# LayerNorm statistics combined on GpSimd instead of VectorE, with the last weight rows loaded twice and a new order of the whole program

## The chip, the cores and the metric

The kernel runs on one core of one Trainium2 chip. The metric is the device time of that core for one execution, in microseconds (us). In the lines of the profile, PE is TensorE's matmuls, PEld its weight loads, DVE is VectorE (called Vector here), ACT is ScalarE, POOL is GpSimd and SP is SyncE, which here only issues DMA. "L783" is line 783 of the kernel.

## The reference

A transformer block on 2048 tokens of width 448, in bf16. The first half is attention over a sliding, dilated window (16 heads of 28, 8 keys at a distance of 2 tokens from each other), the second a gated MLP that mixes tokens with a 2048 x 2048 matrix. Cut to what matters:

```python
def layernorm(x):
    return (x - mean(x)) / sqrt(var(x) + 1e-5)

q, k, v = split(layernorm(A_x) @ A_wqkv)          # 448 -> 3 x 448
logits  = q . k[pos - 2*j] / sqrt(28),  j = 0..7  # masked where pos - 2*j < 0
h       = A_x + (softmax(logits) . v) @ A_wo

z       = gelu(layernorm(h) @ B_w_in)             # 448 -> 1792
z1, z2  = z[:, :896], z[:, 896:]
g       = B_w_sp @ layernorm(z2) + B_b_sp         # mixes the 2048 tokens
out     = h + (z1 * g) @ B_w_out                  # 896 -> 448
```

There are three LayerNorms: LN1 on the input, LN2 on h, and LN3 on z2. The change concerns the first two.

## The kernel before

**Tiles.** The 2048 tokens are 16 blocks of 128. Block u and block u + 8 form unit u, so there are 8 units. In the transposed activations `xh` the first 1024 tokens lie on partitions 0 to 63 and the second 1024 on partitions 64 to 127, each with the 448 channels as seven blocks of 64. A product over 448 channels is therefore seven pairs of 64-row matmuls, one pair member per half, which run side by side on TensorE. So every weight (wqkv, w_in) must lie on both partition halves: it is loaded as three blocks of 128 rows and one of 64 rows, and Vector or ScalarE copy what a half lacks from the other one (`cross`, L569, for V and w_in; the pad copies, L741 to L756, for Q and K, which also spread the heads from 28 to 32 columns).

**A LayerNorm unit** (`ln_unit`, L650) is: `bn_stats` (L656) and `bn_aggr` (L657) on Vector for each of the two blocks; then the reciprocal root `rs`, two operations on GpSimd (add eps, then a power of -1/2; L646, L647) or two on ScalarE (L668, L669); then two normalisations on Vector (L676); then a transpose, either by a DMA on SyncE (L683, LN1 units 0 to 4 and all of LN2) or on TensorE (L692) with an eviction (L700). GpSimd's second operation waits for its first.

`bn_stats` writes six numbers for a row of 448: count, mean and squared deviation of the even elements, and the same of the odd ones. `bn_aggr` combines them into mean and variance.

**Stages.** TensorE first runs 15 filling products on constants (L635). Then q and k are made in chunks of the 1024 paired tokens (L783): chunks 3 and 2 are 128 tokens each (units 7 and 6), chunk 1 is 256 (units 4 and 5), chunk 0 is 512 (units 0 to 3). V (L823) and the attention tiles (nine of 114 tokens, from tile 8 down to 0) follow as their tokens come: logits (L858), exponential on ScalarE (L870), the mask on Vector (L877), row sums (L886), logarithm and scaling on ScalarE (L899, L921), products with V (L911), their eviction with the scaling on Vector (L929), the output product (L964) and the residual addition on Vector (L972), whose result LN2 takes up again. Then come z2 (L984), its gelu on ScalarE (L994), LN3 (L1000 to L1014), z1 (L1028), and to the end the mixing product g (L1064) and the output product (L1093).

**What sets the order.** Nothing is ordered by the hardware or a compiler: the program is a list of tasks (`rs1_4`, `nrm1_12`, `cpk000`, ...), and the table `SEQ` gives for each of the five engines the order in which it issues them. Each engine works its own list in that order and waits at the head of it. `Planner.replay` (L304) steps through the five lists with estimated durations, gives out the eight PSUM banks in that estimated order, and emits the instructions; the class `Sched` adds the semaphores. The planner's constants (durations, DMA rates, what an instruction fetch costs) thus touch the program only through banks and buffers, and through the table.

Of the kernel before, what the change touches and what calls it, by code (L numbers as in the profile page):

```python
# [5 lines left out]
S_TOK = 2048  # L6
# [18 lines left out]
BLK = ((0, 2, 4, 6, 1, 3, 5), (1, 3, 5, 0, 2, 4, 6))  # L25
# [40 lines left out]
)  # L66
NBANKS = 8
NE = 2
NL = 2
NV = 3  # L70
# [125 lines left out]
class Task:  # L196
# [3 lines left out]
    def __init__(self, name, eng, dur, emit, deps=(), acq=(), rel=(), mode=None,  # L200
# [13 lines left out]
        self.setup = 2.0  # L214
        self.waits = []
        self.mark = None
        self.alts = alts
        self.start = self.end = None


# [943 lines left out]
```

## Time and profile before

| | |
|---|---|
| time, three runs | median 241.22 us (241.19 to 241.9) |
| profiled execution | span 241.1 us |
| Vector, share of the span | 59%; 90% or more in 12 of the 40 slices, nine of them from 42 to 96 us |
| GpSimd | 27.1 us busy, 11% |
| DMA | 20.01 MB in 54,628 packets |
| PEclk | 9 (tenths of full speed, 9 is 90% or more) in every slice |

The profile's page has several parts. The first gives the busy time of each engine. The second cuts the span into 40 slices of 6 us and prints the busy share of each engine in tenths, and for DMA also GB/s. The third lists the DMA queues. The fourth is the chain of work that ended last, followed back from the last instruction: each row is a start, a length, and the engine and line, or "issue" where the engine waited for nothing that the profile shows. The fifth gives groups of equal instructions: the row ends in busy time, the mean length of one in ns, and the idle time of the engine just ahead of them. The timeline lists instructions of an engine in order of start: start, length, engine, line, operation, result and operands, and in brackets how long the engine had been idle and what ended that. A row for a tile (for instance `rs`) gives minimum, median and maximum length in ns, then the first and last start. The table by windows gives, for each stretch of time, the busy share of PE and PEld (with the instructions started), then of DVE, ACT and POOL, the granted clock, the share of DMA and its GB/s.

The profiled program has 6691 instructions. Loads take place all through the first half of the span, and DMA is nearly idle for a good part of the second, in which TensorE works on the mixing and output products.

### The profile page before, as it was taken

Reading aid. Unit: us, or ns where it says so; the run is one execution under the profiler, and the core shown is the slowest. Engines: PE = TensorE matmul, PEld = TensorE weight load, DVE = VectorE, ACT = ScalarE, POOL = GpSimd, SP = SyncE. Lnnn points to the kernel's source line nnn. Section 1 sums busy time; section 2 is a strip of 40 time slices with the busy share of each in tenths; the row PEclk is TensorE's granted clock in tenths of the full one; section 3 lists DMA queues with packets and bytes.
Section 4 is the critical chain, followed back from the end, with each engine's and each line's share of the span. In section 5 each row is a group of like instructions: output and inputs, shape, how many; then the busy total and the mean of one; then the engine's idle time right before and its main releaser. Section 6 shows DMA issues by size and latency. Waiting matters only on the chain.

```text
span 241.1 us, 6691 instructions
## 1 busy us (share of the span) xinstructions
PE 234.0 (97%) x3009; PEld 119.8 (50%) x3019; DVE 141.3 (59%) x280; ACT 92.9 (39%) x111; POOL 27.1 (11%) x68
## 2 busy tenths in 40 slices
PE   7898999999999999999999999999999999999995
PEld 2476865455554444454444444444444444444453
DVE  4998954999999999778820050253101436554443
ACT  2898879859899648665630000000000000000000
POOL 6044000002014023105700000000000000000000
PEclk9999999999999999999999999999999999999999
DMA  7927787732303567998535433200000000010122
GB/s 210 331 57 84 117 136 151 140 78 61 44 4 72 108 112 172 181 161 132 113 83 152 90 87 79 52 3 0 0 0 3 0 0 19 19 61 0 38 93 79
DMA packets 54628, 20.01 MB, mean 83 GB/s; under 512 B 46792, under 2 KB 54472, under 8 KB 54600
## 3 DMA queue, kind: packets, MB, share of 16 engines
q1 hardware_dynamic: 53416, 18.61, 37.9%
q10 hardware_dynamic: 1184, 0.98, 1.4%
q8 instruction: 23, 0.38, 0.7%
q14 instruction: 5, 0.04, 0.0%
HBM read 6.37 MB, written 1.84 MB: 34 GB/s over the span
## 4 chain that ended last, share of the span: by engine, by line
PE 85%; DVE 5%; POOL 3%; issue 2%; DMA 2%; ACT 1%; POOLq 1%; ACTq 0%
PE psum L1064 40%; PE psum L783 9%; PE psum L1093 9%; PE psum L984 8%; PE psum L823 5%; PE psum L964 5%; PE psum L1028 4%; PE psum L858 2%; DMA z2p<-in_A_wqkv_dram 2%; POOL rs L647 2%; PE psum L911 1%; DVE x_tm L972 1%; DVE w_in L643 1%; DVE reg L643 1%; PE psum L886 1%
## 5 line engine op out<-in xcount | busy, mean ns | idle before, releaser
L1073 DVE TENSOR_TENSOR ub<-psum,reg 128x512 bf16<-128x512 f32 x28 | 18.9, 688 | 68.4 <-PE psum L1064 66.0
L1064 PE MATMUL psum<-reg,z2p 128*128 128x512 bf16 x220 | 49.4, 379 | 0.2
L1064 PE MATMUL psum<-wspT_lo,z2p 128*128 128x512 bf16 x218 | 48.5, 379 | 0.4 <-DVE z2p L1014 0.2
L1064 PEld LDWEIGHTS psum<-wspT_lo,z2p 128*128 128x128 bf16 x224 | 21.8, 98 | 26.6 <-issue 0.4
L1064 PEld LDWEIGHTS psum<-reg,z2p 128*128 128x128 bf16 x224 | 21.9, 98 | 26.2
L783 PE MATMUL psum<-xh,reg 64*128 64x128 bf16 (+2 forms) x448 | 26.4, 270 | 0.4 <-issue 0.4
L984 PE MATMUL psum<-w_in,xh 64*128 64x448 bf16 x224 | 22.4, 349 | 0.0
L1093 PE MATMUL psum<-reg 128*128 128x448 bf16 (+2 forms) x119 | 22.2, 342 | 0.1
L1028 PE MATMUL psum<-xh,w_in 64*128 64x512 bf16 x196 | 22.0, 376 | 0.0
L656 DVE BATCH_NORM_STATS2 st<-x_tm 128x6 f32<-128x448 bf16 x32 | 19.5, 610 | 3.6 <-DMA x_tm<-in_A_x_dram 3.5
L783 PEld LDWEIGHTS psum<-xh,reg 64*128 64x128 bf16 x448 | 16.8, 94 | 7.9 <-issue 1.4
L641 ACT ACTIVATE reg<-psum 128x896 bf16<-128x896 f32 (+2 forms) x24 | 19.4, 838 | 1.1 <-PE psum L783 0.9
L1000 DVE BATCH_NORM_STATS2 st<-z2p 128x6 f32<-128x448 bf16 x32 | 17.8, 610 | 1.9 <-ACT z2p L994 1.8
L870 ACT ACTIVATE reg<-psum 128x928 bf16<-128x928 f32 x18 | 16.3, 944 | 5.2 <-PE psum L858 5.2
L994 ACT ACTIVATE z2p<-psum 128x896 bf16<-128x896 f32 x16 | 14.2, 918 | 7.6 <-PE psum L984 7.6
L1038 ACT ACTIVATE reg<-psum 128x1024 bf16<-128x1024 f32 x14 | 13.6, 1026 | 8.4 <-PE psum L1028 8.4
L1093 PEld LDWEIGHTS psum<-reg 128*128 128x128 bf16 x119 | 11.4, 98 | 10.4
L646 POOL TENSOR_SCALAR rs<-mv 128x2 f32<-128x2 f32 x19 | 6.5, 342 | 88.9 <-DVE mv L657 72.3
L1103 DVE TENSOR_TENSOR tring<-psum,x_tm 128x448 bf16<-128x448 f32 (+2 forms) x17 | 10.1, 597 | 10.2 <-PE psum L1093 10.0
L984 PEld LDWEIGHTS psum<-w_in,xh 64*128 64x128 bf16 x224 | 10.6, 94 | 10.5 <-issue 0.4
L1028 PEld LDWEIGHTS psum<-xh,w_in 64*128 64x128 bf16 x196 | 9.4, 94 | 11.5 <-ACT reg L1038 0.2
L647 POOL TENSOR_TENSOR rs<-rs,nhalf 128x2 f32<-128x2 f32 x19 | 14.3, 754 | 1.6
(62 smaller groups left out, 202.7 us busy)
## 6 DMA issues: line engine op xcount, KB each, us to landing
x_tm<-in_A_x_dram SPq DMA_DIRECT2D x15, 112.0 KB, 4.9
out_dram<-tring SPq DMA_DIRECT2D x15, 112.0 KB, 1.7
w_in<-in_B_w_in_dram SPq DMA_DIRECT2D x2, 448.0 KB, 4.7
reg<-in_B_w_out_dram SPq DMA_DIRECT2D x1, 784.0 KB, 6.0
z2p<-in_A_wqkv_dram ACTq DMA_DIRECT2D x2, 336.0 KB, 5.5
reg<-in_B_b_sp_dram SPq DMA_DIRECT2D x1, 512.0 KB, 4.6
w_in<-in_B_w_in_dram SPq DMA_DIRECT2D x2, 224.0 KB, 4.7
reg<-in_A_wo_dram SPq DMA_DIRECT2D x4, 98.0 KB
```

What stands on the lines that cost most here:

```text
L641: iss("act", lambda e: e.activation(dst, src, AF.Copy), reads=rd, writes=wr)
L647: iss("pool", lambda e: e.tensor_tensor(dst, dst, nh, ALU.pow), reads=rr + [r_nhalf], writes=rr)
L656: iss("dve", lambda e: e.bn_stats(st[:, b, :], x_tm[:, b, :]), reads=[r_x[b]], writes=[rl[b]])
L783: iss("pe", lambda e, c=c, s=s, gi=gi, lhs=lhs: e.matmul(psum[:, bk[s] * 512 + cw * gi:bk[s] * 512 + cw * gi + cw], lhs, xh[64 * s:64 * s ...
L870: iss("act", lambda e: e.activation(E[:, es[0], 2 * n:2 * n + 2, :], pair_view(lb, 0, 8 * JW), AF.Exp, scale=SCALE), reads=[r_bank[lb[0]], ...
L984: iss("pe", lambda e, k2=k2, c=BLK[s][k2], s=s: e.matmul(psum[:, zb[s] * 512:zb[s] * 512 + D], xh[64 * s:64 * s + 64, c, HX + 128 * u:HX + ...
L994: iss("act", lambda e: e.activation(z2p[:, u:u + 9:8, D * k:D * k + D], pair_view(zb, 0, D), AF.Gelu_apprx_tanh), reads=[r_bank[zb[0]], r_ ...
L1000: iss("dve", lambda e, b=b: e.bn_stats(st3[:, b, k, :], z2p[:, b, D * k:D * k + D]), reads=[r_z2[b][k]], writes=[r_st3[b][k]])
L1028: iss("pe", lambda e, k=k, c=BLK[s][k], s=s: e.matmul(psum[:, bk[s] * 512:bk[s] * 512 + 512], w_in[64 * s:64 * s + 64, k, 128 * f:128 * f ...
L1064: iss("pe", lambda e, b=b: e.matmul(psum[:, gb[0] * 512:gb[0] * 512 + 512], z2p[:, b, 128 * f:128 * f + 128], src[:, b, 512 * (tc % 2):512 ...
L1073: iss("dve", lambda e: e.tensor_tensor(ub[:, us_[0], :], psum[:, gb[0] * 512:gb[0] * 512 + 512], bb[:, 512 * tc:512 * tc + 512], ALU.add), ...
L1093: iss("pe", lambda e, f=f: e.matmul(psum[:, wb[0] * 512 + d0:wb[0] * 512 + d1], z1p[f][:, 128 * m:128 * m + 128], w_out[:, f, d0:d1], star ...
```

## The change

It has four parts.

1. **Statistics.** Vector keeps `bn_stats` for all units, but `bn_aggr` only for units 7 and 6 of LN1 (`AGGR`). For the other six units of LN1 and all eight of LN2, GpSimd combines the six numbers itself: a new function `aggr` of nine operations on 128 x 2 elements, each waiting for the one before. Five combine two tensors (subtract, square, two sums, and the sum of the means), three scale by constants, and the last is the power. So `rs1_0`, `rs1_2` and `rs1_3`, which ScalarE made before with two activations, are GpSimd's too; `rs1_6` is on GpSimd and `rs1_7` on ScalarE.

2. **Weights.** The last 64 rows of each third of wqkv, and of w_in, are loaded twice, once to each partition half. For w_in this is a load of its own over all 1792 columns (`ld_winl`). The cross copies then carry three blocks each way, where one way had four. The four pad copies for Q and K become three: one on all 128 partitions, and one on each half. The order of the channel blocks on the upper half changes with that (`BLK`), and the q and k products read the block that fits their weight.

3. **Constants.** Some memsets move from GpSimd to Vector (pads of Wq, of V, and the zeros under wo); those for the k pads, the ones and the mask band no longer wait for `rs1_7`.

4. **Order.** The planner's constants change, it gets two rules for Vector and GpSimd waiting on each other, and `SEQ` is searched anew. The V products of the first two tiles come ahead of all q and k products (L868 before L828 in the new program, on TensorE's list); x blocks 14, 15, 7 and 6 are loaded first; the weights of V are loaded ahead of those of Q and K; pieces of wo and w_in are loaded later.

The core of the diff (the planner's new durations are left out, and of `SEQ` a line stands for all):

```diff
-BLK = ((0, 2, 4, 6, 1, 3, 5), (1, 3, 5, 0, 2, 4, 6))
+BLK = ((0, 2, 4, 6, 1, 3, 5), (1, 3, 5, 6, 0, 2, 4))
...
-    (23, 29, 26, 28, 31, 24, 27, 25, 30, 55, 48, 85, 87, 73, 86, 330, 384, 366, 348, 402, 420, 438, 456, 341, 413, 395, 359,
+    (26, 31, 29, 27, 28, 88, 90, 30, 89, 44, 58, 51, 76, 70, 64, 82, 330, 384, 348, 366, 420, 456, 402, 438, 395, 359,
...
+AGGR = (7, 6)
+AGT = 2.9
+SPLIT = "q"
...
+        self.blk = 2 if name[:3] in ('nrm', 'cpk', 'cpq') else 0
...
         def w_view(dst, src):
...
-                    (dst[0:64, 3, :], src[384:448], 154.0))
+                    (dst[0:64, 3, :], src[384:448], 200.0), (dst[64:128, 3, :], src[384:448], 200.0))
...
         def cross(name, w, rs, deps, n):
             out = []
-            for h, lo, nb in ((0, 4, 3), (1, 3, 4)):
+            for h in range(2):
                 tk = []
...
+                    copy(tk[0].eng, w[64 * h:64 * h + 64, 4:NC7, :], w[64 - 64 * h:128 - 64 * h, 0:3, :], rs[:-2], [rs[h - 2]])
...
+        def ld_winl():
+            for h in range(2):
+                t_winl.append(dma("sp", "winl%d" % h, lambda e, h=h: e.dma_start(w_in[64 * h:64 * h + 64, 3, :], B_w_in[384:448, :]),
+                                  64 * FH * 4, writes=[r_winl[h]], bw=240.0))
...
+        def aggr(s6, m2, dst, rr):
+            def tt(a, b, c, op):
+                iss("pool", lambda e: e.tensor_tensor(a, b, c, op), reads=rr, writes=rr)
+
+            def ts(a, b, c, d, o1, o2=None):
+                iss("pool", lambda e: e.tensor_scalar(a, b, c, d, o1, o2) if o2 else e.tensor_scalar(a, b, c, None, o1), reads=rr, writes=rr)
+            me, qe, mo, qo = (s6[:, :, n] for n in (1, 2, 4, 5))
+            mean, var = m2[:, :, 0], m2[:, :, 1]
+            tt(var, me, mo, ALU.subtract)
+            tt(var, var, var, ALU.mult)
+            ts(var, var, 0.25 * D, None, ALU.mult)
+            tt(dst, qe, qo, ALU.add)
+            tt(var, var, dst, ALU.add)
+            ts(var, var, 1.0 / D, EPS, ALU.mult, ALU.add)
+            tt(mean, me, mo, ALU.add)
+            ts(mean, mean, 0.5, None, ALU.mult)
+            iss("pool", lambda e: e.tensor_tensor(dst, var, nhalf[:, 0:2], ALU.pow), reads=rr + [r_nhalf], writes=rr)
...
         def ln_unit(u, which, src_deps, ev_deps):
...
+            ag = which == 1 and u in AGGR
...
-                    iss("dve", lambda e: e.bn_aggr(mv[:, b, :], st[:, b, :]), reads=[rl[b]], writes=[rl[b]])
...
+                    if ag:
+                        iss("dve", lambda e: e.bn_aggr(mv[:, b, :], st[:, b, :]), reads=[rl[b]], writes=[rl[b]])
...
-                if tk[0].eng == "pool":
+                if not ag:
+                    aggr(st[:, u:u + 9:8, :], mv[:, u:u + 9:8, :], dst, rr)
+                elif tk[0].eng == "pool":
                     rstd(dst, var, nhalf[:, 0:2], rr)
...
-                for n, (h, q) in enumerate(((0, 0), (0, 1), (1, 0), (1, 1))):
+                for n, (h0, h1, lo, q) in enumerate(((0, 128, 0, 0), (0, 64, 4, 64), (64, 128, 4, 0))):
...
-                                        xh[64 * s:64 * s + 64, c, HX + t0:HX + t0 + cw],
+                                        xh[64 * s:64 * s + 64, b, HX + t0:HX + t0 + cw],
```

**How the lists change.** The rows below are an engine's list in the order of issue: line, operation, result and operands, shape, and how many of them in a row.

ScalarE at its start, before: its loads, then the reciprocal root of unit 7 (L668, L669) and copies of weights (L641).

```order
L553 DMA x_tm<-in_A_x_dram 128x448
L566 DMA z2p<-in_A_wqkv_dram 128x3x448
L566 DMA z2p<-in_A_wqkv_dram 64x448
L566 DMA reg1<-in_A_wqkv_dram 64x448
L566 DMA z2p<-in_A_wqkv_dram 64x448
L508 ACT_TABLE_LOAD
L566 DMA z2p<-in_A_wqkv_dram 128x3x448
L668 ACTIVATE rs1<-mv1,epst 128x2
L669 ACTIVATE rs1<-rs1 128x2
L641 ACTIVATE reg1<-z2p 64x3x8x28
```

In the new program, where they are L712, L713 and L663:

```order
L563 DMA x_tm<-in_A_x_dram 128x448 x2
L518 ACT_TABLE_LOAD
L576 DMA reg1<-in_A_wqkv_dram 64x448
L712 ACTIVATE rs1<-mv1,epst 128x2
L713 ACTIVATE rs1<-rs1 128x2
L663 ACTIVATE reg1<-reg1 64x1344
L663 ACTIVATE xh<-psum 128x7x128 x2
L663 ACTIVATE reg1<-z2p 128x4x8x28
```

ScalarE now issues three loads where it issued six, and its first copies are half of V's weights (64x1344) and the evictions of both transposed units (`xh<-psum`).

GpSimd from the first `rs` on, before: two roots, constants for the k and q pads and the mask band, a third root, and then the constants for the row sums.

```order
L646 TENSOR_SCALAR rs1<-mv1 128x2
L647 TENSOR_TENSOR rs1<-rs1,nhalf 128x2
L646 TENSOR_SCALAR rs1<-mv1 128x2
L647 TENSOR_TENSOR rs1<-rs1,nhalf 128x2
L714 MEMSET reg2 128x8x2
L715 MEMSET reg2 128x4x14
L716 MEMSET reg2 128x8x2
L717 MEMSET reg2 128x8x2
L723 MEMSET mband 128x58
L725 AFFINE_SELECT mband<-mband 64x58
L727 AFFINE_SELECT mband<-mband 64x58
L725 AFFINE_SELECT mband<-mband 64x58
```

In the new program the constants are done, and from the first root (unit 6, with Vector's aggregation) on there stand:

```order
L668 TENSOR_SCALAR rs1<-mv1 128x2
L669 TENSOR_TENSOR rs1<-rs1,nhalf 128x2
L674 TENSOR_TENSOR mv1<-st1 128x2
L674 TENSOR_TENSOR mv1<-mv1 128x2
L677 TENSOR_SCALAR mv1<-mv1 128x2
L674 TENSOR_TENSOR rs1<-st1 128x2
L674 TENSOR_TENSOR mv1<-mv1,rs1 128x2
L677 TENSOR_SCALAR mv1<-mv1 128x2
L674 TENSOR_TENSOR mv1<-st1 128x2
L677 TENSOR_SCALAR mv1<-mv1 128x2
L688 TENSOR_TENSOR rs1<-mv1,nhalf 128x2
L674 TENSOR_TENSOR mv1<-st1 128x2
```

From the third row on this is unit 4 in nine operations, and units 5, 1, 2, 3 and 0 of LN1 follow in the same way, then LN2's units 7, 4, 6, 5, 2, 0, 3 and 1.

Vector inside attention, where LN2 begins, before: statistics (L656) and aggregations (L657) of LN2 among masks (L877), additions (L972), normalisations (L676) and L929 steps.

```order
L929 TENSOR_TENSOR reg2<-psum,reg3 128x2x8x57
L676 TENSOR_SCALAR tring<-x_tm,mv2,rs2 128x2x7x32
L972 TENSOR_TENSOR x_tm<-psum,x_tm 128x2x448
L877 TENSOR_TENSOR reg3<-reg3,mband 128x1856
L972 TENSOR_TENSOR x_tm<-psum,x_tm 128x2x448
L929 TENSOR_TENSOR reg2<-psum,reg3 128x2x8x57
L656 BN_STATS st2<-x_tm 128x6
L657 BN_AGGR mv2<-st2 128x2
L656 BN_STATS st2<-x_tm 128x6
L657 BN_AGGR mv2<-st2 128x2
L656 BN_STATS st2<-x_tm 128x6
L657 BN_AGGR mv2<-st2 128x2
```

In the new program, in the same stretch, where these lines are L697, L922, L1018, L720 and L974:

```order
L922 TENSOR_TENSOR reg3<-reg3,mband 128x1856
L1018 TENSOR_TENSOR x_tm<-psum,x_tm 128x2x448 x2
L974 TENSOR_TENSOR reg2<-psum,reg3 128x2x8x57
L697 BN_STATS st2<-x_tm 128x6 x2
L922 TENSOR_TENSOR reg3<-reg3,mband 128x1856
L697 BN_STATS st2<-x_tm 128x6
L974 TENSOR_TENSOR reg2<-psum,reg3 128x2x8x57
L697 BN_STATS st2<-x_tm 128x6
L720 TENSOR_SCALAR tring<-x_tm,mv2,rs2 128x2x7x32
L697 BN_STATS st2<-x_tm 128x6
L922 TENSOR_TENSOR reg3<-reg3,mband 128x1856
L720 TENSOR_SCALAR tring<-x_tm,mv2,rs2 128x2x7x32
```

The aggregations are gone, and a normalisation (`tring<-x_tm,mv2,rs2`) now stands behind a chain on GpSimd that begins when the second statistics of its unit are done.

More of the change, by code (lines that the diff above doesn't have):

```diff
@@ L197 @@
     __slots__ = ("name", "eng", "dur", "emit", "deps", "acq", "rel", "mode", "epoch",
-                 "nbytes", "start", "end", "nmm", "alts", "bw", "setup", "waits", "mark")
+                 "nbytes", "start", "end", "nmm", "alts", "bw", "setup", "waits", "mark", "blk")
     def __init__(self, name, eng, dur, emit, deps=(), acq=(), rel=(), mode=None,
@@ L321, in replay @@
                     continue
-                at = max([free[e]] + [d.end + (self.SAME if d.eng == e else self.LAT)[d.eng] for d in t.deps])
+                at = max([act_at if e == "act" and t.nbytes else free[e], pool_to if e == "dve" and t.blk == 2 else 0.0] + [d.end + (self.SAME if d.eng == e else self.LAT)[d.eng] for d in t.deps])
                 for p, n, h in t.acq:
@@ L354, in replay @@
             t.start = now
-            free[e] = now + dur + extra
+            free[e] = max(free[e], now + dur) if t.nbytes else now + dur + extra
+            if e == "act":
+                act_at = now + dur if t.nbytes else now
+            if e == "pool" and t.blk == 1:
+                pool_to = now + dur
             if t.nbytes:
@@ L528, in dve4x, with dma @@
             return (190.0 + 0.26 * n) / 1000.0
-        def dma(eng, name, fn, nbytes, deps=(), reads=(), writes=(), rel=(), store=False, issue=0.62, bw=335.0, after=(), setup=1.0, both=False):
+        def dma(eng, name, fn, nbytes, deps=(), reads=(), writes=(), rel=(), store=False, issue=0.48, bw=335.0, after=(), setup=1.0, both=False):
             def em():
@@ L606, in bass_sequential_preLN__sliding_local_dilated__mixer_gmlp__prompt_kernel, with cst @@
         add("c_tab", "act", 0.01, lambda: None, epoch=0)
-        def cst(name, fns, dur, eng="pool", deps=()):
+        def cst(name, fns, dur, eng="pool", deps=(), dve=None):
+            tk = []
             def em():
                 for fn, rd, wr in fns:
-                    iss(eng, fn, reads=rd, writes=wr)
-            return add(name, eng, dur, em, deps=deps)
-        c_warm = cst("c_warm", [(lambda e: e.memset(warm[:], 1.0), [], [r_warm])], 0.5)
-        c_eps = cst("c_eps", [(lambda e: e.memset(epst[:], EPS), [], [r_eps])], 0.1)
-        c_nhalf = cst("c_nhalf", [(lambda e: e.memset(nhalf[:], -0.5), [], [r_nhalf])], 0.1)
+                    iss(tk[0].eng, fn, reads=rd, writes=wr)
+            t = add(name, eng, dur, em, deps=deps, alts={"pool": dur, "dve": dve} if dve else None)
+            tk.append(t)
+            t.blk = 1
+            return t
+        c_warm = cst("c_warm", [(lambda e: e.memset(warm[:], 1.0), [], [r_warm])], 0.55, dve=0.25)
+        c_eps = cst("c_eps", [(lambda e: e.memset(epst[:], EPS), [], [r_eps])], 0.15)
+        c_nhalf = cst("c_nhalf", [(lambda e: e.memset(nhalf[:], -0.5), [], [r_nhalf])], 0.15)
         c_ident = cst("c_ident", [
@@ L939, in bass_sequential_preLN__sliding_local_dilated__mixer_gmlp__prompt_kernel @@
                 writes=[r_wo[hh]], deps=[c_wo0]))
+        ld_winl()
         ld_win(1)
```

75 lines of the change are left out of this document (39 added, 36 removed), and 59 rows, old and new, of the table SEQ.

## Prediction

> **What bounds the kernel now.** I read the profile's first part first, then the chain of work that ended last, then the timeline by engine.
>
> ```profile
> span 241.1 us, 6691 instructions
> PE 234.0 (97%) x3009; PEld 119.8 (50%) x3019; DVE 141.3 (59%) x280; ACT 92.9 (39%) x111; POOL 27.1 (11%) x68
> ```
>
> TensorE is busy for 97% of the span, and the chain says from when to when its real work sets the end:
>
> ```profile
> 9.86 0.96 PE psum L783 x28
> ...
> 34.84 3.13 PE psum L783 x28
> ...
> 80.41 1.69 PE psum L964 x8
> ...
> 120.73 10.74 PE psum L1064 x49
> ...
> 238.61 0.31 DVE tring L1103
> ```
>
> From 9.86 us (the first q product, L783) to 238.61 TensorE is the chain, but for few short waits; the two longest of them that no engine explains are shown below. The last 117.9 us (L1064, L1093) hold the same products in the new kernel, so a gain or loss must come before 120.73: an earlier start, fewer gaps, or new waits.
>
> **The start.**
>
> ```profile
> 1.36 6.22 PE L635 MATMUL psum<-warm 128*128 128x512 bf16 x15 [1.36 <-POOL warm L614]
> ...
> 7.78 0.56 PE L692 MATMUL psum<-ident,tring 128*128 128x128 bf16 x7 [0.19 <-DVE tring L676]
> ...
> 9.10 0.62 DVE L643 COPY xh<-psum 128x896 bf16<-128x896 bf16 x1
> ...
> 10.52 0.92 ACT L641 ACTIVATE xh<-psum 128x896 bf16<-128x896 bf16 x1
> ```
>
> ```profile
> L641 ACT ACTIVATE reg<-z2p 64x1344 bf16<-64x1344 bf16 x1 | 1.3, 1322 | 0.0
> ```
>
> ```profile
> 2.17 0.43 SPq L566 DMA_DIRECT2D reg<-in_A_wqkv_dram  x1
> ```
>
> ```profile
> DMA to landing us min/median/max: 4.8/5.6/6.0
> ```
>
> The filling products hold TensorE to 7.58 us. Then come unit 7's transposes (0.56), their eviction on Vector (0.62, begun late, at 9.10) and q. The new order has V first, with both transposed units evicted on ScalarE (0.92, the row at 10.52). If ScalarE is free when the transposes end at about 8.2, V starts at 9.15. But ScalarE must first copy half of the V weights (64x1344, 1.32). Their large load is the fourth issue on SyncE's queue, as the load in the 2.17 row was; weight loads landed 4.8 to 6.0 us after their issue, so at 7.0 to 8.2. Only loads of 56 and 112 KB stand ahead of it, so I take 7.0: copy to 8.3, eviction to 9.25, V at 9.3. That is 0.55 us earlier; the bounds are 0.7 earlier and 0.6 later. The new memsets on Vector stand ahead of its first statistics, for which Vector waits until 3.13 (row below): nothing.
>
> **The two gaps.** In TensorE's timeline, two waits are marked "issue":
>
> ```profile
> 13.53 3.22 PE L783 MATMUL psum<-xh,reg 64*128 64x128 bf16 x108
> 17.11 2.63 PE L783 MATMUL psum<-xh,reg 64*128 64x128 bf16 x88 [0.37 <-issue]
> 19.67 0.56 PE L692 MATMUL psum<-ident,tring 128*128 128x128 bf16 x7
> 20.17 0.44 PE L858 MATMUL psum<-reg 32*64 32x58 bf16 x32
> 21.32 0.71 PE L858 MATMUL psum<-reg 32*64 32x58 bf16 x64 [0.71 <-issue]
> ```
>
> ```profile
> q8 instruction: 23, 0.38, 0.7%
> ```
>
> ```profile
> 12.00:13.00 1.00, 1.00 (x28) 0.61 (x24) 0.97 (x3) 1.00 (x2) 0.00 (x0) 1.00 1.10 237
> ...
> 15.00:16.00 1.00, 1.00 (x44) 1.00 (x39) 0.95 (x3) 1.00 (x3) 0.16 (x1) 1.00 0.00 0
> ```
>
> Between the gaps stand 88 + 7 + 32 = 127 matmuls, each with a weight load: some 256 instructions. The instruction queue moved 0.38 MB in 23 packets, 16.5 KB each, which is 65 bytes for each of 256. So I read both gaps as TensorE waiting for its next piece of program. DMA is full to 13 us (share 1.10) and empty at 15, so the first piece came behind the loads, and the second could only follow the first. The new SyncE list puts some 0.5 MB (part of w_in, two pieces of wo) behind the first transposing DMA; at the 237 GB/s of that row the burst ends 2 us sooner. I take both gaps as gone: 0.37 + 0.71 = 1.08 us (bounds 0 and 1.08).
>
> [...]
>
> **What GpSimd takes over.** Vector loses 28 aggregations (14 units of two), GpSimd gets nine operations for two in each unit:
>
> ```profile
> L657 DVE BATCH_NORM_AGGREGATE mv<-st 128x2 f32<-128x6 f32 x32 | 5.8, 182 | 1.1
> L616 POOL MEMSET nhalf<- 128x2 f32 x1 | 0.1, 104 | 0.1
> ```
>
> ```profile
> L676 DVE TENSOR_SCALAR tring<-x_tm,mv,rs x32: 362/388/399, 6.5 to 96.5; 128x448 bf16<-128x448 bf16 x32
> ```
>
> ```profile
> 110.90 0.22 POOL L646 TENSOR_SCALAR rs<-mv 128x2 f32<-128x2 f32 x1 [11.55 <-DVE mv L1006]
> 111.20 0.70 POOL L647 TENSOR_TENSOR rs<-rs,nhalf 128x2 f32<-128x2 f32 x1
> 111.99 0.22 POOL L646 TENSOR_SCALAR rs<-mv 128x2 f32<-128x2 f32 x1
> ```
>
> Vector saves 28 x 0.18 = 5.1 us. GpSimd's small operation starts 0.30 before the next (110.90 to 111.20), the power 0.79 (111.20 to 111.99). Three of the nine are such operations, one is the power. The other five read two tensors without a power, which no row has. Their bounds are the memset of as many elements (0.10, with the same 0.08 between operations 0.18) and the power (0.79). The nearest rows are the memset and the one-tensor operation (0.30), far from the power; I take the middle of the two, 0.24. A unit then takes 5 x 0.24 + 3 x 0.30 + 0.79 = 2.9 us (bounds 2.6 and 5.6) where it took 1.1, undisturbed. And it is disturbed:
>
> ```profile
> 13.69 0.58 DVE L643 COPY reg<-z2p 64x1792 bf16<-64x1792 bf16 x1
> 13.87 0.50 POOL L646 TENSOR_SCALAR rs<-mv 128x2 f32<-128x2 f32 x1 [8.47 <-DVE mv L657]
> ```
>
> ```profile
> 55.45 1.09 DVE L877 TENSOR_TENSOR reg<-reg,mband 128x1856 bf16<-128x1856 bf16 x1
> 55.62 1.00 POOL L646 TENSOR_SCALAR rs<-mv 128x2 f32<-128x2 f32 x1 [33.98 <-DVE mv L657]
> ```
>
> A copy (SBUF to SBUF) and a masking product on Vector held a 0.22 us operation of GpSimd until 0.08 to 0.10 after their own end. If such an instruction of length B starts in the middle of a 0.30 step, the next small operation starts 0.15 later and ends at B + 0.08 in place of 0.37: B - 0.29 is lost, 0.80 for a mask, 0.29 for this copy, 0.08 for a normalisation of 0.37. [...]
>
> *First place: the end of the first LayerNorm.*
>
> ```profile
> DMA to landing us min/median/max: 3.4/3.7/4.1
> ```
>
> ```profile
> 3.13 0.63 DVE L656 BATCH_NORM_STATS2 st<-x_tm 128x6 f32<-128x448 bf16 x1 [3.13 <-DMA x_tm<-in_A_x_dram]
> ```
>
> In the new order GpSimd takes units 4, 5, 1, 2, 3, 0 in a row. Unit 4's statistics end near 9.3: Vector's first four pairs from 3.13 to 6.1, four normalisations and a V copy, with a wait for GpSimd's first power, to 8.1, two statistics of 0.6. Beside the chains stand two masks (7 and 8), seven copies (half of them of the length above, half shorter: 0.2 each) and ten normalisations: 1.6 + 1.4 + 0.8 = 3.8, of which the quarter that falls on a power, already running, is free: 2.8, or 0.47 a chain. Six chains of 3.37 end at 29.5. Unit 0's normalisations add 0.7, the transposing DMA lands 3.4 to 3.7 later: 33.75. TensorE comes to the 512-token q products, the first to need unit 0, at 34.84 (the L783 of the chain) - 0.55 - 1.08 = 33.2. So it waits some 0.6 us. Bounds: 0, and 4.8 if each of the eight operations takes 0.35; the power's price I leave out as too far.
>
> *Second place: the second LayerNorm inside attention.*
>
> ```profile
> L929 DVE TENSOR_TENSOR reg<-psum,reg 128x912 bf16<-128x912 f32 x9 | 11.1, 1232 | 3.6 <-ACT reg L921 3.6
> L877 DVE TENSOR_TENSOR reg<-reg,mband 128x1856 bf16<-128x1856 bf16 x9 | 9.9, 1113 | 3.3 <-ACT reg L870 3.3
> L972 DVE TENSOR_TENSOR x_tm<-psum,x_tm 128x896 bf16<-128x896 f32 x8 | 8.6, 1079 | 0.4 <-PE psum L964 0.3
> ```
>
> ```profile
> 51.85 1.09 DVE L972 TENSOR_TENSOR x_tm<-psum,x_tm 128x896 bf16<-128x896 f32 x1
> ```
>
> ```profile
> 79.12 1.23 DVE L929 TENSOR_TENSOR reg<-psum,reg 128x912 bf16<-128x912 f32 x1 [0.30 <-ACT reg L921]
> ```
>
> From 52.94 to 80.35 Vector's list was worked off, and TensorE's output product waited for its last step (80.41, above). In the new order the same stretch holds six L929 steps, five masks, five additions, ten statistics, six normalisations and one V eviction (as large as an addition): 7.4 + 5.6 + 5.4 + 6.0 + 2.2 + 1.1 = 27.7, no shorter than these 27.4: what the aggregations gave up is filled again. Every wait of Vector here is TensorE's. Unit 4's chain starts together with mask 1, so it takes 1.2 for its first operation, then 7 x 0.26 + 0.79: 3.8 us. Vector comes to its normalisation after mask, statistics, L929 step and statistics, 3.55 us. That is 0.25 of waiting; queued behind it are mask 0 and the last two L929 steps, for which the output products of units 0 and 1 wait. Unit 6's chain adds as much. I take 0.5 (bounds 0 and 1.5). The output products of units 0 and 1 change places, and one z2 product goes ahead of them; I cost that at nothing, since both wait for the same Vector steps, and at up to 0.5 if that is wrong.
>
> Copies of w_in: four on Vector become three there and one on ScalarE, which has 60% of the span idle; the pad copies are three for four. Nothing, while TensorE's banks let it run ahead.
>
> **The sum.** 241.1 - 0.55 - 1.08 + 0.6 + 0.5 = 240.6 for this execution, whose span is 0.1 below the median of 241.22: **240.7 us**, which is no change, since 0.3% (0.72 us) is about what a measurement of this kernel can tell.
>
> **Rivals.**
>
> *GpSimd keeps up.* If the five operations cost as little as the memset, a chain is 2.6 us, disturbed 3.07: no wait at the first place, 0 to 0.5 at the second: 239.6 to 240.1. It holds when a chain's mean, disturbance included, is under 3.27 us (33.2 - 3.55 - 0.7 - 9.3 in six). For it: GpSimd's rows stand at 0.22 under statistics and PSUM evictions, which are most of Vector's time.
>
> *GpSimd becomes the bound.* If the five cost 0.30 like the one-tensor operation, a chain is 3.2, disturbed 3.67: the six end at 31.3, unit 0 lands at 35.55 and TensorE waits 2.4; with 1.0 at the second place: 241.1 - 1.63 + 3.4 + 0.1 = 243.0, slower. It decides from 3.5 us a chain on. For it: reading two tensors should not be cheaper than reading one. Against: a normalisation starts within 0.1 us of the next chain's first operation, too late to hold it.
>
> *The start or the gaps don't change.* Late V weights or other causes of "issue" give back up to 1.6 us, but what TensorE comes later to unit 0 it waits less there: 240.7 + 0.5 to 1.1, 241.2 to 241.8.
>
> **How the numbers follow.** My forecast has 0.32 (its own range, 240.3 to 241.3, puts 0.08 of that under 240.5), GpSimd keeping up 0.31, GpSimd as the bound 0.31, the unchanged start 0.06. So faster 0.39, same 0.30, slower 0.31. The range takes in both rivals at the times worked out for them: 239.6 to 243.0.
>
> **What would show it.** Right: the first 64x448 product at 9.3; no "issue" gap before 22 us; GpSimd's chains 3.3 to 3.45 us on average from unit 4 to unit 0; a TensorE wait near 33 us ahead of the 128x512 q products; and one near 79 for a Vector L929 step. Wrong: chains under 3.27 with no wait at 33 us (faster), chains over 3.5 (slower), or an idle stretch elsewhere, above all between 82 and 121 us, where I expect none.

## The result, and the profile after

The changed kernel takes **251.99 us** (median of four runs, 250.07 to 254.51), the kernel before 241.56 beside it. The ratio, which leaves out the slowest of these four runs (over 1.5% above the fastest), is 1.0408 (95% interval 1.0362 to 1.0454): slower by 4.1%, some 9.9 us, where the prediction had 240.7 us and a range to 243.0.

The head of the page, with the granted clock by slices of 6.3 us:

```profile
span 250.9 us, 6778 instructions
...
PE 238.1 (95%) x3019; PEld 121.4 (48%) x3019; DVE 136.2 (54%) x256; ACT 91.7 (37%) x101; POOL 51.5 (21%) x169
...
PEclk9999997999979999999999999999999999999999
```

TensorE is busy for 238.1 us where it was busy for 234.0, with the same products: part of its work ran slower. Two slices show it, a 7 in the one from 37.6 us on and another in the one from 69.0. TensorE's timeline, where the bracket gives the idle time ahead of a row and what ended it:

```profile
8.83 2.85 PE L868 MATMUL psum<-reg,xh 64*64 64x448 bf16 x56
...
24.36 0.39 PE L903 MATMUL psum<-reg 32*64 32x58 bf16 x24 [0.88 <-issue]
...
33.38 0.73 PE L956 MATMUL psum<-reg 64*32 64x58 bf16 x64
37.23 4.88 PE L828 MATMUL psum<-xh,reg 64*128 64x512 bf16 x28 [3.12 <-issue]
...
58.65 0.46 PE L903 MATMUL psum<-reg 32*64 32x58 bf16 x31 [1.64 <-issue]
59.05 1.52 PE L868 MATMUL psum<-reg,xh 64*64 64x448 bf16 x28
60.49 0.46 PE L903 MATMUL psum<-reg 32*64 32x58 bf16 x32
60.88 1.52 PE L868 MATMUL psum<-reg,xh 64*64 64x448 bf16 x28
62.33 0.39 PE L931 MATMUL psum<-reg,ones 64*32 64x464 bf16 x8
62.65 1.69 PE L1010 MATMUL psum<-reg 128*128 128x448 bf16 x8
64.27 0.39 PE L931 MATMUL psum<-reg,ones 64*32 64x464 bf16 x8
64.48 0.73 PE L956 MATMUL psum<-reg 64*32 64x58 bf16 x64
65.14 0.71 PE L903 MATMUL psum<-reg 32*64 32x58 bf16 x48
67.27 0.32 PE L903 MATMUL psum<-reg 32*64 32x58 bf16 x16 [1.42 <-issue]
67.52 4.88 PE L1010 MATMUL psum<-reg 128*128 128x448 bf16 x16
...
79.96 3.20 PE L1010 MATMUL psum<-reg 128*128 128x448 bf16 x16
...
85.89 1.08 PE L956 MATMUL psum<-reg 64*32 64x58 bf16 x112 [0.80 <-DVE x_tm L1018]
...
130.22 5.14 PE L1110 MATMUL psum<-wspT_lo,z2p 128*128 128x512 bf16 x23
```

The last part (g and out) begins at 130.22 where it began at 120.73, 9.5 us later; it takes as long as before within 0.3 us. The terms, in us:

| term | worked out from | us |
|---|---|---|
| earlier start | 8.83 for 9.86 | -1.0 |
| early waits marked issue | 0.88 for 0.37 + 0.71 | -0.2 |
| wait ahead of the 512-token q products | row at 37.23 | +3.1 |
| these 28 products slow | 4.88 for 3.20 | +1.7 |
| two more waits marked issue | 1.64 + 1.42 | +3.1 |
| 16 output products slow | 4.88 (67.52) for 3.20 (79.96) | +1.7 |
| wait for an addition on Vector | row at 85.89 | +0.8 |
| sum | | 9.2 of 9.5 |

The rest is small waits and switches between kinds of products. Why those products are slow, the windows of 1 us tell; the column behind POOL is the granted clock:

```profile
38.00:39.00 1.00, 1.00 (x8) 0.36 (x4) 0.00 (x0) 0.00 (x0) 0.00 (x0) 0.50 0.23 53
...
41.00:42.00 1.00, 1.00 (x11) 0.34 (x6) 0.00 (x0) 1.00 (x2) 0.00 (x0) 1.00 0.96 353
```

After the wait of 3.12 us the clock is half for some 3.4 us (37.5 to 40.9), and again from 68.2 to 71.6, after the wait of 1.42. Behind the wait of 1.64 it stays at 1.00.

The wait of 3.12 us is named issue, but its place is the first product that needs unit 0. GpSimd's timeline from the first chain to the end of the last, and Vector behind it:

```profile
10.04 0.27 POOL L674 TENSOR_TENSOR mv<-st 128x2 f32<-128x2 f32 x1 [2.60 <-DVE st L697]
...
25.95 1.03 POOL L677 TENSOR_SCALAR mv<-mv 128x2 f32<-128x2 f32 x1
...
29.72 0.20 POOL L674 TENSOR_TENSOR rs<-st 128x2 f32<-128x2 f32 x1
29.99 0.20 POOL L674 TENSOR_TENSOR mv<-mv,rs 128x2 f32<-128x2 f32 x1
...
31.14 0.72 POOL L688 TENSOR_TENSOR rs<-mv,nhalf 128x2 f32<-128x2 f32 x1
```

```profile
9.33 0.63 DVE L697 BATCH_NORM_STATS2 st<-x_tm 128x6 f32<-128x448 bf16 x1 [0.62 <-DMA x_tm<-in_A_x_dram]
...
25.78 1.13 DVE L922 TENSOR_TENSOR reg<-reg,mband 128x1856 bf16<-128x1856 bf16 x1 [0.56 <-ACT reg L915]
...
31.89 0.70 DVE L720 TENSOR_SCALAR tring<-x_tm,mv,rs 128x448 bf16<-128x448 bf16 x2 [2.34 <-POOL rs L688]
```

```profile
24.41 9.44 SPq L727 DMA_TRANSPOSE xh<-tring  x4
```

Six chains from 10.04 to 31.86 are 3.64 us each. Vector stood 2.34 us for the last of them, normalised unit 0 until 32.59, and the last of four transposing DMAs left SyncE by 33.85. TensorE had come to the place at 34.11 (the end of the row at 33.38) and went on at 37.23, 3.4 us after that issue.

### The profile page after: what moved, and what is told of

Its sections match the earlier page's. It is cut to its first block, busy times and chain, and to the rows that moved or that the text cites. A ratio compares the mean times of both kernels' runs of the same rounds, so it can differ in the third digit from the quotient of the medians.

```text
span 250.9 us, 6778 instructions
## 1 busy us (share of the span) xinstructions
PE 238.1 (95%) x3019; PEld 121.4 (48%) x3019; DVE 136.2 (54%) x256; ACT 91.7 (37%) x101; POOL 51.5 (21%) x169
## 4 chain that ended last, share of the span: by engine, by line
PE 83%; POOL 5%; issue 5%; DVE 2%; DMA 2%; SPq 2%; ACT 0%; POOLq 0%
PE psum L1110 39%; PE psum L828 9%; PE psum L1139 8%; PE psum L1074 8%; PE psum L1030 8%; PE psum L1010 4%; PE psum L868 3%; PE psum L903 2%; POOL mv L674 2%; DMA x_tm<-in_A_x_dram 2%; POOL mv L677 2%; PE psum L956 1%; POOL rs L688 1%; SPq L576 1%; DVE st L697 1%
## 5 line engine op out<-in xcount | busy, mean ns | idle before, releaser
L1110 PE MATMUL psum<-wspT_lo,z2p 128*128 128x512 bf16 x224 | 49.2, 379 | 0.0
L828 PE MATMUL psum<-xh,reg 64*128 64x128 bf16 (+2 forms) x448 | 28.0, 279 | 3.2 <-issue 3.1
L828 PEld LDWEIGHTS psum<-xh,reg 64*128 64x128 bf16 x448 | 17.4, 96 | 11.6 <-issue 5.5
L663 ACT ACTIVATE reg<-psum 128x1024 bf16<-128x1024 f32 (+2 forms) x23 | 19.2, 862 | 9.2 <-PE psum L828 9.1
L697 DVE BATCH_NORM_STATS2 st<-x_tm 128x6 f32<-128x448 bf16 x32 | 19.2, 613 | 2.5 <-DMA x_tm<-in_A_x_dram 2.5
L674 POOL TENSOR_TENSOR mv<-st 128x2 f32<-128x2 f32 x28 | 7.0, 251 | 50.6 <-DVE st L697 48.2
L720 DVE TENSOR_SCALAR tring<-x_tm,mv,rs 128x448 bf16<-128x448 bf16 x32 | 11.5, 388 | 8.9 <-POOL rs L688 8.8
```

Of the source, the lines that this page charges most:

```text
L663: iss("act", lambda e: e.activation(dst, src, AF.Copy), reads=rd, writes=wr)
L697: iss("dve", lambda e: e.bn_stats(st[:, b, :], x_tm[:, b, :]), reads=[r_x[b]], writes=[rl[b]])
L828: iss("pe", lambda e, c=c, b=BLK[s][c], s=s, gi=gi, lhs=lhs: e.matmul(psum[:, bk[s] * 512 + cw * gi:bk[s] * 512 + cw * gi + cw], lhs, xh[6 ...
L1110: iss("pe", lambda e, b=b: e.matmul(psum[:, gb[0] * 512:gb[0] * 512 + 512], z2p[:, b, 128 * f:128 * f + 128], src[:, b, 512 * (tc % 2):512 ...
```

## The experiments

Twelve runs, in three groups of four, each timed beside the kernel before; the ninth is the kernel before itself. They are called by their number here (the fourth kernel, the second). Line numbers differ a little between them (L828, L829, L831 and L832 are the same q and k products).

**Which part loses the time.** Three kernels keep the new code and lists and give the aggregation back to Vector (the planner's durations stay, so lists and banks are the same); a fourth moves only the aggregation in the kernel before.

```diff
             ag = which == 1 and u in AGGR
+            on_v = which == 1                 # e1;  True in e2;  which == 2 or ag in e3
...
-                    if ag:
+                    if on_v:
                         iss("dve", lambda e: e.bn_aggr(...
...
-                if not ag:
+                if not on_v:
                     aggr(...
```

LN1 on Vector:

> The changed kernel with its lists as they are, but LN1's aggregation back on Vector for all units, so that GpSimd does only the two old operations there. Theory A (GpSimd's row of six chains comes late to unit 0; TensorE's wait of 3.12 us, the low clock behind it and the new places of the instruction fetches all follow from that): no wait ahead of the 512-token products, clock 1.0 there, fetch gaps mostly gone, 241 to 243 us. Theory B (the new lists themselves, with their transposing loads and small products, starve TensorE of instructions): the 3.1 us wait goes and its 1.7 us of low clock, but some 3 us of fetch gaps with their low clock stay, 245 to 247 us. Theory C (LN2's chains inside attention are the loss): 250 us.

Everything on Vector:

> As before, and LN2's aggregation on Vector too, so that only loads, constants and lists are new. A: 240.0 to 242, since then only the earlier start is left and Vector has 2.5 us more to do inside attention. B: 245 to 247. C: 241, with the first experiment at 250.

LN2 on Vector:

> Only LN2's aggregation back on Vector; LN1's chains stay on GpSimd. A: still 249 to 251, the 3.1 us wait stays. B: 250. C: 241 to 245.

And in the kernel before, `aggr` wherever GpSimd had the root:

```diff
-                    iss("dve", lambda e: e.bn_aggr(mv[:, b, :], st[:, b, :]), ...
+                    if tk[0].eng != "pool":
+                        iss("dve", lambda e: e.bn_aggr(mv[:, b, :], st[:, b, :]), ...
...
                 if tk[0].eng == "pool":
-                    rstd(dst, var, nhalf[:, 0:2], rr)
+                    aggr(st[:, u:u + 9:8, :], mv[:, u:u + 9:8, :], dst, rr)
```

> The kernel before with its own lists and loads, and only the aggregation moved: GpSimd's nine operations for LN1 units 4, 5 and 1 and for all of LN2; units 0, 2 and 3 keep Vector's aggregation and ScalarE's root. A: no six chains in a row, so no wait for unit 0; 241 to 243, with small waits for chains of LN2. B: no change, 241.2. C (LN2's chains are dear wherever they are): 244 or more.

| kernel | median us | ratio to before (95%) |
|---|---|---|
| changed | 251.99 | 1.0408 (1.0362 to 1.0454) |
| LN1 on Vector | 247.95 | 1.0263 (1.0197 to 1.0328) |
| all on Vector | 247.67 | 1.0255 (1.0200 to 1.0310) |
| LN2 on Vector | 250.44 | 1.0374 (1.0326 to 1.0422) |
| before, with GpSimd's aggregation | 249.92 | 1.0363 (1.0332 to 1.0394) |

Theory C falls: LN2's chains are worth at most 1.5 us in the new lists, and the intervals allow for none. Theory A holds for some 4 us, with LN1's chains: without them the wait ahead of the 512-token products is 0.39.

```profile
34.71 3.20 PE L829 MATMUL psum<-xh,reg 64*128 64x512 bf16 x28 [0.39 <-issue]
```

But 6.3 us remain with everything on Vector (247.67, just above theory B's 245 to 247). And A and B both missed the fourth: GpSimd's aggregation alone, in the old lists, costs 8.6 us. Only theory C allowed for that (244 or more); the eleventh and the twelfth run below divide it. In the second kernel (all on Vector) the losses have these rows, in TensorE's and Vector's timelines and in the windows:

```profile
14.02 4.21 PE L829 MATMUL psum<-xh,reg 64*128 64x128 bf16 x140 [0.67 <-DVE reg L665]
...
46.92 0.39 PE L932 MATMUL psum<-reg,ones 64*32 64x464 bf16 x8 [1.00 <-DVE reg L665]
...
62.61 0.42 PE L904 MATMUL psum<-reg 32*64 32x58 bf16 x16 [1.41 <-issue]
```

```profile
42.16 1.08 DVE L665 COPY w_in<-w_in 64x2688 bf16<-64x2688 bf16 x1 [3.11 <-DMA w_in<-in_B_w_in_dram]
43.25 2.16 DVE L923 TENSOR_TENSOR reg<-reg,mband 128x1856 bf16<-128x1856 bf16 x2
...
45.64 1.22 DVE L665 CAST reg<-psum 128x1024 bf16<-128x1024 f32 x1
```

```profile
63.00:64.00 1.00, 1.00 (x7) 0.40 (x4) 0.00 (x0) 0.92 (x2) 0.00 (x0) 0.50 0.20 42
```

Copies of weights on Vector come late (0.67), which they do not in the changed kernel, where Vector has fewer aggregations ahead of them. Vector stands 3.1 us at its first copy of w_in until the load has landed, with two masks and an eviction behind it, for which TensorE waits 1.0. And the wait marked issue, 1.41 here, follows the 1496th matmul, as the 1.42 in the changed kernel does, with half clock behind it.

**What the waits marked issue are, and the half clock.** In the changed kernel's rows above, 31 + 28 + 32 + 28 + 8 + 8 + 8 + 64 + 48 = 255 matmuls stand between the waits of 1.64 and 1.42 us: with a weight load each, 510 instructions, about two of the pieces of 256 that the prediction reckons from the instruction queue (0.38 MB in 23 packets in this kernel too). So I moved a long product ahead of the place (fifth kernel, on the second), and in the kernel before put short products ahead of it (seventh). The sixth fills the wait for unit 0 in the changed kernel with products on constants. The eighth is the fifth with Vector's copy of w_in later.

```diff
 # fifth: TensorE's list of the second kernel
-  ... mml2_00 mml2_01 mml2_10 mml2_11 mmy5 mmy4 ...
+  ... mml2_00 mml2_01 mmy5 mml2_10 mml2_11 mmy4 ...
 # sixth, in the q and k products of the changed kernel
+                        if (p, t0, g0) == ("q", 0, 3):
+                            for _ in range(14):
+                                iss("pe", lambda e: e.matmul(psum[:, bk[0] * 512:bk[0] * 512 + 512], warm[:, 0:128], warm[:, :]), ...
 # seventh, in the products with V of the kernel before
-                    for sg in (2 * qd, 2 * qd + 1):
+                    for sg in (2 * qd, 2 * qd + 1) * (2 if i == 4 else 1):
 # eighth: the fifth, and in Vector's list
-  ... evk0_1 cpw0_1 mask6 mask5 xpad evq0_1 cpw1_1 ...
+  ... evk0_1 mask6 mask5 xpad evq0_1 cpw0_1 cpw1_1 ...
```

> The second experiment's kernel (all aggregation on Vector) with one move in TensorE's list: the output product of unit 5 (8 matmuls, 1.6 us) goes ahead of the last two groups of logits of tile 2, so that TensorE comes 1.6 us later to the matmul at which it waited 1.41 us, the 1497th. Theory B1 (that wait is for a piece of program, and the half clock of 3.4 us behind it follows from the wait): the wait goes or shrinks under 0.3 us, the clock stays at 1.0, 1.4 + 1.7 = 3 us less. Rival (the wait is for an engine or a DMA that the profile doesn't name, and the half clock comes on its own): no change within 0.5 us, the wait stands where the unit's logits stand.

It took 246.65 us, 1.0 less than the second kernel and not 3, and the intervals of the two overlap. The wait behind the 1496th matmul is gone. But the profiled execution has one of 1.00 behind the 1241st, with half clock behind that one:

```profile
54.72 0.46 PE L906 MATMUL psum<-reg 32*64 32x58 bf16 x31 [1.00 <-issue]
```

```profile
56.00:57.00 1.00, 1.00 (x16) 0.52 (x12) 1.00 (x2) 0.16 (x1) 0.00 (x0) 0.50 0.31 77
```

So the rival falls (the wait doesn't belong to the unit's logits); the eighth kernel below, with the same move, has no wait there either. The wait at 54.72 is not the old one moved: the product was moved at 63.1, 8 us later, and the same place has 1.64 us in the changed kernel, 0.31 in the first, 0.54 in the third and no such wait in the second. It varies, then, with the kernel or the execution. Three of the four runs of the fifth kernel had a granted clock of 0.999 or 1.0, so hardly any half clock, and only one of the second kernel's four. What the move itself was worth can't be separated from that.

> The kernel before, with the 64 products of V of tile 4 issued twice, which costs TensorE 0.55 us of work. Theory B1 (in this stretch TensorE runs at the rate at which its program arrives, and the kernel before is just in time for it): a wait marked issue of 1 to 1.5 us opens near 61 us, perhaps with 3.4 us of half clock behind it: 1.5 to 3.7 us slower. Rival (program arrives early enough, the doubled work costs only itself): 0.5 to 0.6 us slower, no new wait.

It took 244.09 us, ratio 1.0131 (1.0077 to 1.0185), 2.7 to 3.2 us more for 0.55 us of work. Its timeline has two new waits, the first behind the 1495th matmul and the second 256 later, without half clock in this execution:

```profile
58.89 0.72 PE L823 MATMUL psum<-reg,xh 64*64 64x448 bf16 x9 [1.30 <-issue]
...
67.51 0.25 PE L858 MATMUL psum<-reg 32*64 32x58 bf16 x5 [0.66 <-issue]
```

That is B1's forecast, in the old lists and the old code: sixty-four short products more, and the kernel before has two such waits, 1.30 and 0.66 us, where the ninth run has none.

> The changed kernel, with 14 filling products on constants (about 3 us) at the place where TensorE waits 3.12 us for unit 0. Theory A1 (the idle time of TensorE halves its clock for some 3.4 us): the 28 products behind it take 3.2 us in place of 4.88, and the kernel is 1.5 to 2 us faster, though 28 more instructions are to be fetched. Rival (the low clock has another cause, such as the products' own kind or the load on the memory at that time): the products still take 4.9 us and the time doesn't fall.

It took 250.35 us, 1.6 less than the changed kernel; the ratio is 1.0369 (1.0347 to 1.0391), and its interval overlaps with that of the changed kernel. The rows settle it: filled, then 28 products at full speed (granted clock 1.00 in each window of 1 us from 33 to 41).

```profile
34.06 3.20 PE L826 MATMUL psum<-warm 128*128 128x512 bf16 x14
37.19 3.20 PE L832 MATMUL psum<-xh,reg 64*128 64x512 bf16 x28
```

A1 holds: 4.88 became 3.20 when TensorE did not stand still. The delay as such stays; filling products stand in its place. The wait behind the 1496th matmul is there too, and longer, 1.99 for 1.42, while the one behind the 1241st is gone:

```profile
65.10 0.63 PE L907 MATMUL psum<-reg 32*64 32x58 bf16 x30 [1.99 <-issue]
```

This row says most about what these waits are. In the changed kernel the wait stands ahead of the last 16 of 64 logits (67.27); with 14 matmuls more ahead of it, it stands ahead of the last 30 of the same 64. It keeps its place in the count of instructions and not in the work, as a wait for a piece of program would. That it is one remains an inference: the view of the DMA queues shows the packets of the instruction queue (in the changed kernel one between 55.9 and 56.0 us and one between 64.6 and 65.0, and none within the waits that ended at 58.65 and 67.27), but not which engine's program a packet holds.

> As the fifth experiment, and Vector's first copy of w_in goes behind the eviction of the 512-token q product. In the second experiment Vector stood 3.1 us at that copy until its load of w_in had landed, with two masks and the eviction behind it, and TensorE waited 1.0 us for the eviction. If that copy is the cause: the 1.0 us goes, 0.7 to 1.2 us less than the fifth experiment. If not (the masks or ScalarE are late anyway): the same as the fifth.

It took 246.38 us, ratio 1.0217 (1.0194 to 1.0240). The wait for the eviction (1.0 in the second kernel, 0.86 in the fifth) is gone: from 40.6 to 51 us the products run on with one wait of 0.16. But the time is that of the fifth kernel within its interval, 0.3 less where 0.7 to 1.2 was forecast, and a wait of 0.40 for Vector opens behind. The copy was the cause of that wait; what it was worth was not to be seen here.

**The kernel before once more, the old lists with the new code, and the aggregation by halves.**

> The kernel before, unchanged, profiled once more. In every kernel here whose profiled execution has a time of its own, that time is 1.7 us over its span; by that the shown profile of before, with a span of 241.1, belongs to an execution of some 242.8, 1.4 over the median. Theory: its two waits marked issue (0.37 and 0.71 us) stand in that execution alone; this profile has neither and a span of 239.4 to 240.0. Rival: they belong to the kernel, and the span is 241 again.

The span is 239.3, and the profiled execution took 241.05 us. TensorE's table of waits (in total, times, longest, in us) has these three rows and one of 0.2 for an addition, and no issue at all:

```profile
PE psum L635 <- POOL warm L614: 1.4, 1, 1.4
PE psum L692 <- DVE tring L676: 0.8, 1, 0.8
PE psum L964 <- DVE mv L657: 0.4, 1, 0.4
```

So the two waits on which the prediction built belong to one execution. Here the first q product began at 9.42, so the gain of the new start is 0.6 against such an execution. The last part began at 118.69, 11.5 us ahead of the changed kernel's, and the terms of the table above then make 10.7 of these 11.5 (0.6 in place of 1.0 for the start, and the wait of 0.88 in full).

```diff
 # tenth: new code, all aggregation on Vector, the old lists by name
+  wq1 -> wq1 wq2;  wv1 -> wv1 wv2;  wk1 -> wk1 wk2;  win0_2 -> winl0;  win1_2 -> winl1
+  cpq001 -> cpq0_0;  cpq010 -> cpq0_1;  cpq011 -> cpq0_2;  cpk010 -> cpk0_0;  ...
 # eleventh: the fourth for LN1 alone;  twelfth: for LN2 alone
+                    if not (which == 1 and tk[0].eng == "pool"):      # which == 2
+                        iss("dve", lambda e: e.bn_aggr(...
...
+                if which == 1 and tk[0].eng == "pool":      # which == 2
                     aggr(...
+                elif tk[0].eng == "pool":
+                    rstd(dst, var, nhalf[:, 0:2], rr)
```

> The new code with Vector's aggregation for all units, and the lists of the kernel before: each task stands where its counterpart stood (the doubled loads behind their fellows, the three pad copies in the places of three of the four). Theory B (the new lists lose what the second experiment still loses, 6.3 us): 241 to 242. Rival (the new loads, the 128-row pad copies or the weights' new blocks lose it): 244 to 248.

It took 243.68 us, ratio 1.0081 (1.0048 to 1.0113), between the two forecasts: 2.0 us of the 6.3 stay, 4.3 go with the old lists. No wait marked issue is left in TensorE's table. Of the 2.0, 1.1 stands at the start (the first q product at 10.52 for 9.42): ScalarE issues three loads more ahead of its table load (which starts at 5.52, for 3.58 in the first profile of before) and its root (6.82 for 5.46), Vector's normalisations begin later (7.39, for 6.24 in the ninth run), and TensorE waits:

```profile
5.52 1.28 ACT L519 ACT_TABLE_LOAD   x1 [5.52 <-issue]
...
6.82 0.30 ACT L713 ACTIVATE rs<-mv,epst 128x2 f32<-128x2 f32 x1
```

```profile
8.45 0.56 PE L737 MATMUL psum<-ident,tring 128*128 128x128 bf16 x7 [2.19 <-DVE tring L721]
```

The doubled loads are not free where ScalarE issues them, 1.1 us here; the new lists avoid just that by giving them to SyncE.

> The kernel before, with GpSimd's nine operations for LN1 units 4, 5 and 1 alone. In the fourth experiment, with LN2 as well, TensorE waited 2.36 us for unit 5, and 249.9 us was the time. If that start is what costs: 244 to 246, and the rest of the 8.5 us belongs to LN2. If each chain costs alike (3 of 11): 243.5.

> The kernel before, with GpSimd's nine operations for LN2 alone. If the start costs most: 243 to 245. If LN2 inside attention, where Vector works without a pause, costs most: 245 to 248, with Vector waiting for GpSimd ahead of normalisations and TensorE waiting for Vector.

Both took 245.95 us, each within the higher of its two forecasts: the ratios are 1.0192 (1.0162 to 1.0222) and 1.0183 (1.0153 to 1.0212), some 4.6 us for three chains of LN1 and as much for eight of LN2, together a little over the 8.6 of the fourth kernel. With LN1, TensorE waits 2.31 us for unit 5, with half clock behind it; with LN2, Vector waits for GpSimd and TensorE for Vector. The rows of the twelfth, Vector's and then TensorE's:

```profile
67.15 1.13 DVE L898 TENSOR_TENSOR reg<-reg,mband 128x1856 bf16<-128x1856 bf16 x1 [0.63 <-ACT reg L891]
70.03 0.40 DVE L697 TENSOR_SCALAR tring<-x_tm,mv,rs 128x448 bf16<-128x448 bf16 x1 [1.75 <-POOL rs L666]
```

```profile
71.48 0.44 PE L879 MATMUL psum<-reg 32*64 32x58 bf16 x32 [1.63 <-DVE x_tm L993]
```

No kernel here beats the kernel before.

## Why the prediction was wrong

**The two gaps** (1.08 us taken as gone) is the step that failed in kind. Their nature, TensorE waiting for program, is an inference that the sixth and the seventh kernel support: such waits keep their place in the count of instructions. But that they would vanish with less traffic in the first 16 us was argued from one execution of before, in which they happened to be; another has none. The question was not asked where else such waits can stand. They stood behind the 1241st and the 1496th matmul, where short products of 58 columns stand close together; the new list puts the same work in another order there, and 1.64 + 1.42 us of waits with 1.7 of half clock came of it. With the old lists in the same code (tenth) the profile has none of these waits, though five of the nine runs had half clock somewhere, as the last section shows.

**The first place** (0.6 us) is the step that was mis-sized: 3.12. The mechanism is the one described. Its terms: the chains began 0.74 later, since the second statistics of unit 4 waited for their input (9.33, where 8.7 was reckoned); they took 3.64 each and not 3.37, 1.6 us in all; from the last normalisation to TensorE's product 4.6 us passed, 1.1 more than the landing of 3.4 to 3.7; and TensorE came 0.9 later. That is 0.6 + 0.74 + 1.6 + 1.1 - 0.9 = 3.1. The price of the unseen operation was near: GpSimd's operations on two tensors took 0.20 us, a step 0.27 to 0.28 (29.72 to 29.99), so an undisturbed chain is 8 x 0.28 + 0.79 = 3.0 for the 2.9 taken. What was short is the disturbance: a mask beside a chain cost what was said (1.03 for 0.22, the row at 25.95), but 0.64 a chain came together and not 0.47. The slow rival had the chain almost exactly, 3.67, and then stopped at a wait of 2.4.

**What no case contained** is the half clock: that a wait of TensorE can cost more than itself. It put 1.7 us on top of the wait of 3.1 and 1.7 on top of that of 1.4, and no row of the profile of before could show it, since no wait there is longer than 0.71 us once the products run.

**The second place** (0.5 us) came out at 0.8, by the mechanism described in its first half only. Unit 4's chain took 3.8 us as reckoned, and Vector waited 0.16 for it where 0.25 was reckoned. Unit 6's chain, reckoned the same, was held in its middle by the next mask, took 4.2 and let Vector wait 1.03:

```profile
80.44 1.23 POOL L677 TENSOR_SCALAR mv<-mv 128x2 f32<-128x2 f32 x1
```

```profile
83.92 0.40 DVE L720 TENSOR_SCALAR tring<-x_tm,mv,rs 128x448 bf16<-128x448 bf16 x1 [1.03 <-POOL rs L688]
```

What stood behind it was an addition and not an L929 step, and products with V waited for it (0.80, the row at 85.89) and not an output product. The first kernel, which keeps these chains, has the same wait (0.84); the third, which does not, has none for Vector there.

**The start** (0.55 earlier) is 0.6 against an execution like the median. **Copies of w_in at nothing** was wrong in the lists without chains: TensorE did not run ahead of the eviction that stood behind such a copy (1.0 us). **The pad copies** cost 0.67 there.

That Vector would gain nothing inside attention was right, but too mild. In the old lists, where Vector loses nothing else, GpSimd's chains cost 8.6 us although Vector saves 11 x 2 aggregations of 0.18: the chain's 3.0 us stand between statistics and normalisation in place of one aggregation (0.18) and GpSimd's two operations (1.1), and everything behind the normalisation in Vector's list waits (in the twelfth kernel Vector waited for GpSimd's root six times, 10.0 us in all).

## What to carry to other kernels

Work taken off a busy engine is no gain if the next step of that engine waits for it elsewhere: compare the latency of the detour with what stands between, place by place, before counting the time saved. Where TensorE runs many short products, look for waits that no engine explains (1.64 and 1.42 us here), and profile twice before you build on a short one (0.37 and 0.71 us stood in one profile of before and not in the next). And price a wait of TensorE like those measured here, 1.00 to 3.12 us, at up to 1.7 us above itself; if it can't be avoided, filling products can keep the clock, as they did in the one place where they were tried.

## What the runs showed of the hardware

The half clock lasts about 3.4 us (37.5 to 40.9 and 68.2 to 71.6 in the changed kernel) and follows some waits and not others of the same length. The fourth and the eleventh kernel wait 2.35 and 2.31 us ahead of the same seven transposes; a window of 1 us behind each, with the clock as the third number from the right:

```profile
23.00:24.00 1.00, 1.00 (x60) 0.75 (x52) 0.84 (x3) 1.00 (x2) 0.70 (x4) 1.00 0.06 16
```

```profile
23.00:24.00 1.00, 1.00 (x16) 0.46 (x12) 0.19 (x2) 1.00 (x2) 0.75 (x4) 0.50 0.02 8
```

Waits of 1.00 (fifth kernel), 1.41, 1.42 and 3.12 us had it behind them; one of 1.64, and one of 1.00 in the second kernel, had not. So it followed a wait of 1.00 us in one execution and not one of 2.35 in another. What decides was not tried.

Whether it comes is at least a part of why the runs of the changed kernel spread over 4.4 us and those of before beside them over 0.8. Half clock for 3.4 us takes 0.007 off the mean clock of a run of some 246 us (an estimate from these two numbers), so by this estimate the granted clock of a run tells how often it had it. The changed kernel's four runs took 250.07 us at 0.993, 251.38 and 252.59 at 0.986, and 254.51 at 0.973. Of the tenth kernel's nine runs the four at 1.0 took 242.3 to 243.1 us, the five at 0.992 or 0.993 took 243.7 to 244.6. In the fourth and the twelfth kernel the clock does not sort the runs, so something else varies too.

The waits marked issue stand behind the same matmuls, counted from the start of the program, in several kernels: the 1241st, the 1496th (1495th in the seventh) and, in the seventh, the 1751st. They lie 255 or 256 apart, which with a weight load each is 510 or 512 instructions. Not every execution of a kernel shows them: one profile of before had two such waits, the next none.
